# The first tap of each gate convolution: GpSimd replaced by VectorE as the planner's second choice

## The chip, the cores and the metric

One core of a Trainium2 chip runs the kernel. The metric is device time in microseconds for one execution. Engines: TensorE (PE; its weight loads are PEld), VectorE (DVE), ScalarE (ACT), GpSimd (POOL), and SyncE (SP), which issues the DMAs.

## What is computed

Attention with a local window of 96 positions and 8 global keys (2 batches, 8 heads, 768 positions, head size 64), and behind it two gated blocks with short convolutions along the sequence:

```python
x = attention(q, k, v)                        # [2, 768, 512]
# block 1: causal convolution of 5 taps over x
gate_pre = sum(conv_w[k] * x_padded[:, k:k + S, :] for k in range(5))
y = (sigmoid(gate_pre) * (x @ w_val)) @ w_out
# block 2: centred convolution of 3 taps over the hidden values
h = maximum(y @ w_in, 0.0)                    # d_ff = 1024
conv_out = sum(conv_w2[k] * h_padded[:, k:k + S, :] for k in range(3))
out = (h * sigmoid(conv_out)) @ w_out2
```

## The kernel before, in words

Channels lie on partitions, positions along the free dimension. The gated blocks are worked in four chunks, two for each batch (`PARTS`, lines 33 and following: 400 and 368 columns; 384 in the second block). For each chunk `hidden_inputs` splits x into a high and a low part (`gx`) and makes the four gates of block 1 (`z`), `values` multiplies by `w_val` and gates, `hidden` multiplies by the product of `w_out` and `w_in` (made on the chip in `weights`), and `gated` makes the eight gates of block 2 (`z2`) and the split operand `g2` of `project`. Every matmul of the blocks is three passes over split operands (`mm3`, lines 253 to 255); `split_ops` makes the high part on ScalarE (line 244) and the low part on VectorE (line 246).

`conv_gate` is called for both convolutions. Its first tap is a multiplication with one weight for each channel, `z = w0 * src`; each further tap adds `wk * src(k)` on VectorE (line 706), and a tanh on ScalarE (line 708) ends it. There are 4 x 4 first taps over x (tile names `z<-x,cw`) and 4 x 8 over h (`z<-h,cw`), 48 in all. Line 701 is the first tap on ScalarE, line 702 on GpSimd.

Nothing here is ordered by hand. Each step is put into a `Plan` with a cost for each engine that may do it. `lay` is a list scheduler: it goes forward in modelled time, and a step with several engines is taken by the one on which it would end first by the costs (`here`); a rank from a backward pass decides among ready steps. `issue` repeats backward and forward passes six times, keeps the pass with the earliest modelled end, and issues all steps in that order; each engine then runs its own steps strictly in that order and waits on semaphores. Costs and order are fixed when the kernel is built.

```python
def here(w, e):
    ends = {o: max(free[o], est[w]) + us for o, (us, _) in w.ways.items()}
    return back or min(ends, key=ends.get) == e
```

Other steps that the text names: scores (line 493), softmax on VectorE and ScalarE (504, 509), the probabilities' scaling on VectorE, GpSimd or ScalarE (530, 533, 536), their transposes on TensorE (563) and copies out of PSUM (567, 573), their product with v (588), the rounding of raw weights to f32 (272, 274 on GpSimd, 279, 282), the product of weights (337), the gate of block 1 (759), relu into h (800) with its edge columns from GpSimd (794 to 805), and the gate of block 2 (819).

Of the kernel before, what the change touches and what calls it, by code (L numbers as in the profile page):

```python
# [14 lines left out]
ALU = mybir.AluOpType  # L15
# [69 lines left out]
class Plan:  # L85

    LAG = {"PE": 0.2, "ACT": 0.15, "DVE": 0.15, "POOL": 0.15, "SP": 0.0, "AHEAD": 0.0}
    START = {"DVE": 0.4, "ACT": 1.2, "SP": 6.3}  # L90
# [130 lines left out]
def act_us(n, sbuf=True, scaled=False, sums=False):  # L221
    return 0.05 + 0.000834 * n + 0.042 * sbuf + 0.092 * scaled + 0.093 * sums


def dve_us(n, scaled=False):
    return 0.069 + 0.001042 * n + 0.061 * scaled
# [6 lines left out]
def pool_us(n):  # L233
    return 0.17 + 0.0013 * n
# [27 lines left out]
def to_f32(c, dst, raw, n, bufs, reads, token):  # L262
# [5 lines left out]
    def whole(): return high().bitcast(F32)  # L268
    def bits(): return dst().bitcast(I32)
# [3 lines left out]
    pl.add(  # L273
        "POOL", pool_us(n), lambda: nc.gpsimd.tensor_scalar(whole(), whole(), 0.0, 1.0, ALU.mult, ALU.mult),  # L274
        bufs, reads + [token], [tail],
# [120 lines left out]
def head_ways(c, n, out, d, h):  # L396

    nc, k = c.nc, -slope(h) / QKSCALE
    return {
        "POOL": (0.02 + pool_us(n), lambda: nc.gpsimd.tensor_scalar(out(), d, k, 1.0, ALU.mult, ALU.mult)),  # L400
        "ACT": (act_us(n), lambda: nc.scalar.activation(out(), d, AF.Copy, scale=k)),
# [35 lines left out]
def fast_attention(c, ap):  # L437
# [35 lines left out]
    def held(d, ts):  # L473
        return [d[t] for t in ts if t in d]

    for t in range(nt):
# [7 lines left out]
        for half in range(2):  # L484
# [40 lines left out]
            four = [("p", t, h) for h in range(4 * half, 4 * half + 4)]  # L525
            pl.add("POOL", 0.12, guard, [st], four, [("r", t, half)])
            pl.add("DVE", 0.2, invert, [st], [], [("r", t, half)])
            for h in range(4 * half, 4 * half + 4):
# [6 lines left out]
                def on_act(h=h, st=st, w=p[h], nk=nk):  # L535
# [3 lines left out]
                    "DVE", 0.22 + 0.00052 * nk, on_dve, [p[h], st], [("r", t, half)], [("p", t, h)],  # L539
                    POOL=(0.2 + pool_us(nk), on_pool), ACT=(act_us(nk, True, True), on_act),  # L540
                )
# [6 lines left out]
        if i == 0:  # L548
            pl.add("POOL", 0.4, first_keys, held(kq, [t]), [("kq", t)], ["gl"])
        elif i < NT - 1:  # L550
# [145 lines left out]
def conv_gate(c, z, width, src, n, w, taps, bufs, reads, token):  # L696


    nc, pl = c.nc, c.plan
    pl.add(  # L700
        "ACT", act_us(n, True, True), lambda: nc.scalar.activation(z(), src(0), AF.Copy, scale=w()[:, 0:1]), bufs, reads, [token],  # L701
        POOL=(pool_us(n), lambda: nc.gpsimd.tensor_scalar(z(), src(0), w()[:, 0:1], 1.0, ALU.mult, ALU.mult)),  # L702
    )
    for k in range(1, taps):
        def tap(k=k):
            nc.vector.scalar_tensor_tensor(z(), src(k), w()[:, k : k + 1], z(), ALU.mult, ALU.add)  # L706
        pl.add("DVE", dve_us(n, True), tap, bufs, reads, [token])
    pl.add("ACT", act_us(n), lambda: nc.scalar.activation(z(), z(), AF.Tanh, scale=0.5), bufs, [], [token])  # L708


def hidden_inputs(c, b, ch):


    nc, ring = c.nc, c.ring
    t0, n = PARTS[ch]
    xt = [("x", i) for i in range(max(0, t0 - K1 + 1) // P, (t0 + n - 1) // P + 1)]
    gx, z = [], []
    for d in range(NC1):
        g = ring["gx"].new()
        split_ops(  # L720
            c, lambda g=g: g.t[:, 0, :n], lambda g=g: g.t[:, 1, :n], lambda d=d: c.x[:, d, XP + t0 : XP + t0 + n],
            n, [g], xt, ("gx", b, ch, d),
        )
        gx.append(g)
    for d in range(NC1):
        zz = ring["z"].new()

        def src(k, d=d):
            return c.x[:, d, XP + t0 - K1 + 1 + k : XP + t0 - K1 + 1 + k + n]

        conv_gate(
            c, lambda zz=zz: zz.t[:, :n], CW, src, n, lambda d=d: c.c1w[:, :, d], K1, [zz], xt + ["cw"], ("z", b, ch, d)
        )
        z.append(zz)
    c.inputs[b, ch] = gx, z
# [73 lines left out]
def gated(c, b, ch, f, h):  # L809

    nc, pl = c.nc, c.plan
    z, g = c.ring["z2"].new(), c.ring["g2"].new()
    tk, zt = [("h", b, ch, f), ("h", b, ch, f, "edge")], ("z2", b, ch, f)
    conv_gate(
        c, lambda: z.t, CH, lambda k: h.t[:, k : k + CH], CH, lambda: c.c2w[:, :, f], K2, [z, h], tk + ["cw"], zt
    )

    def gate():
        nc.vector.scalar_tensor_tensor(z.t, z.t, 1.0, h.t[:, 1 : 1 + CH], ALU.add, ALU.mult)  # L819

    pl.add("DVE", dve_us(CH), gate, [z, h], tk, [zt])
    split_ops(c, lambda: g.t[:, 0], lambda: g.t[:, 1], lambda: z.t, CH, [g, z], [zt], ("g2", b, ch, f))
    c.g2.setdefault((b, ch), []).append(g)
# [223 lines left out]
```

## Time and profile before

| | |
|---|---|
| median of 3 runs | 284.13 us (283.84 to 284.21) |
| the profiled execution | 283.84 us, of which the span is 281.9 us |
| TensorE busy, share of the span | 269.6 us, 96% |
| VectorE | 232.2 us, 82% |
| ScalarE | 194.8 us, 69% |
| GpSimd | 90.0 us, 32% |
| mean granted clock of TensorE | 0.999 |

The span runs from the first instruction of the program to the last one's end. A share is an average over stages with different limits, so the stages are to be read one by one. Matmuls overlap and their ends are modelled, so a matmul's busy time is longer than its step from start to start.

### The profile page before, as it was taken

The numbers are of one execution on the slowest core, as the hardware profiler recorded it, in microseconds if no ns is written. First come the engines' busy times: TensorE is split into PE (matmuls) and PEld (weight loads), VectorE is DVE, ScalarE is ACT, GpSimd is POOL, SyncE is SP. The second block draws the span as 40 slices with busy tenths as digits, with TensorE's granted clock in tenths as the row PEclk, the third lists the DMA queues.
The fourth block names the chain that finished last, engine by engine and source line by source line (L and its number), as shares of the span: only waits on it lengthen the run. The fifth ranks groups of instructions, "written<-read, shape, count | busy, mean of one in ns | idle before, by whom it ended". The sixth has DMA issues, their size and how long they took to land.

```text
span 281.9 us, 5430 instructions
## 1 busy us (share of the span) xinstructions
PE 269.6 (96%) x1832; PEld 226.3 (80%) x1832; DVE 232.2 (82%) x587; ACT 194.8 (69%) x496; POOL 90.0 (32%) x199
## 2 busy tenths in 40 slices
PE   2889999999999999999999999999999999999993
PEld 2767675655458989999999999889999988899883
DVE  3989999999999999999999999999984654357600
ACT  2999989998678999886797456883473254544520
POOL 4635746346353336533256001140411000002000
PEclk9999999999999999999999999999999999999999
DMA  5983877446733431003300000100000020000121
GB/s 165 356 346 97 277 243 237 141 140 216 227 87 140 144 127 49 9 2 116 121 0 0 3 0 0 40 37 1 37 2 0 0 77 37 37 1 2 38 112 49
DMA packets 10420, 26.17 MB, mean 93 GB/s; under 512 B 1424, under 2 KB 2704, under 8 KB 10384
## 3 DMA queue, kind: packets, MB, share of 16 engines
q1 hardware_dynamic: 9968, 25.22, 26.4%
q10 hardware_dynamic: 416, 0.52, 0.5%
q8 instruction: 16, 0.26, 0.4%
q14 instruction: 20, 0.16, 0.2%
HBM read 22.59 MB, written 3.15 MB: 91 GB/s over the span
## 4 chain that ended last, share of the span: by engine, by line
PE 72%; DVE 21%; issue 3%; ACT 1%; DVEq 1%; POOL 0%
PE s L254 8%; PE s L255 8%; PE s L253 8%; PE f L253 7%; PE f L254 7%; PE f L255 7%; DVE p L504 5%; PE t L563 4%; PE x L588 4%; PE s L493 4%; DVE z L706 3%; DVE raw L279 3%; PE t L255 2%; PE x L255 2%; PE x L253 2%
## 5 line engine op out<-in xcount | busy, mean ns | idle before, releaser
L706 DVE SCALAR_TENSOR_TENSOR z<-h,cw,z 128x384 f32<-128x384 f32 x64 | 40.7, 642 | 12.8 <-ACT z L701 11.6
L509 ACT ACTIVATE p<-p,st 128x256 f32<-128x256 f32 (+1 forms) x96 | 46.0, 482 | 3.8 <-DVE st L504 2.9
L708 ACT ACTIVATE z<-z 128x384 f32<-128x384 f32 (+2 forms) x48 | 24.8, 523 | 26.3 <-DVE z L706 26.0
L706 DVE SCALAR_TENSOR_TENSOR z<-x,cw,z 128x400 f32<-128x400 f32 (+1 forms) x64 | 40.5, 666 | 0.1
L254 PE MATMUL s<-w,g 128*128 128x512 f32 (+1 forms) x104 | 39.2, 377 | 0.0
L255 PE MATMUL s<-w,g 128*128 128x512 f32 (+1 forms) x104 | 39.2, 377 | 0.0
L253 PE MATMUL s<-w,g 128*128 128x512 f32 (+1 forms) x104 | 39.1, 376 | 0.0
L337 PE MATMUL f<-w,w 128*128 128x512 f32 x64 | 31.9, 607 | 0.1
L563 PEld LDWEIGHTS t<-ident,p 128*128 128x128 f32 x176 | 20.0, 141 | 14.0 <-issue 4.3
L504 DVE CUSTOM_DVE_ANT_0 p<-s,B 128x256 f32<-128x256 f32 x80 | 30.9, 412 | 0.3 <-PE s L493 0.3
L563 PE MATMUL t<-ident,p 128*128 128x128 f32 x176 | 28.6, 281 | 2.1 <-ACT pts L567 1.0
L533 POOL TENSOR_SCALAR p<-p,st 128x256 f32<-128x256 f32 (+1 forms) x38 | 24.8, 658 | 12.4 <-DVE st L523 11.4
L253 PE MATMUL f<-gg,Wh 128*128 128x400 f32 (+1 forms) x80 | 27.7, 347 | 0.0
L255 PE MATMUL f<-gg,Wl 128*128 128x400 f32 (+1 forms) x80 | 27.0, 338 | 0.0
L254 PE MATMUL f<-gg,Wh 128*128 128x400 f32 (+1 forms) x80 | 27.0, 338 | 0.0
L702 POOL TENSOR_SCALAR z<-h,cw 128x384 f32<-128x384 f32 x11 | 9.7, 883 | 51.6 <-DVE z L706 31.0
L274 POOL TENSOR_SCALAR raw<-raw 128x512 f32<-128x512 f32 x24 | 19.4, 810 | 16.8 <-ACT m L272 8.6
L255 PEld LDWEIGHTS s<-w,g 128*128 128x128 f32 x104 | 19.5, 188 | 3.9
L246 DVE TENSOR_TENSOR g<-z,g 128x384 fp32r<-128x384 f32 x32 | 17.7, 564 | 5.9 <-ACT g L244 5.9
L253 PEld LDWEIGHTS s<-w,g 128*128 128x128 f32 x104 | 19.5, 188 | 2.8
L254 PEld LDWEIGHTS s<-w,g 128*128 128x128 f32 x104 | 19.5, 188 | 2.8
L244 ACT ACTIVATE g<-z 128x384 fp32r<-128x384 f32 x32 | 16.3, 518 | 7.8 <-DVE z L819 4.7
(126 smaller groups left out, 662.2 us busy)
## 6 DMA issues: line engine op xcount, KB each, us to landing
raw<-in_moe_w_out_dram SPq DMA_DIRECT2D x12, 512.0 KB, 3.4
raw<-in_moe_w_in_dram SPq DMA_DIRECT2D x8, 512.0 KB, 4.9
k<-in_kq_dram SPq DMA_DIRECT2D x7, 512.0 KB, 4.5
v<-in_v_dram SPq DMA_DIRECT2D x11, 256.0 KB, 4.2
out_dram<-o SPq DMA_DIRECT2D x11, 256.0 KB, 2.0
raw<-in_moe_w_val_dram SPq DMA_DIRECT2D x4, 512.0 KB, 3.4
kq<-in_kq_dram SPq DMA_DIRECT2D x3, 512.0 KB, 4.6
v<-in_v_dram SPq DMA_DIRECT2D x8, 64.0 KB, 3.0
```

What stands on the lines that cost most here:

```text
L246: "DVE", dve_us(n), lambda: nc.vector.tensor_tensor(lo(), src(), hi().bitcast(F32), ALU.subtract),
L253: nc.tensor.matmul(out, lh, rh, start=first, stop=False)
L254: nc.tensor.matmul(out, lh, rl, start=False, stop=False)
L255: nc.tensor.matmul(out, ll, rh, start=False, stop=last)
L274: "POOL", pool_us(n), lambda: nc.gpsimd.tensor_scalar(whole(), whole(), 0.0, 1.0, ALU.mult, ALU.mult),
L337: nc.tensor.matmul(ps.t, big["wot"].t.bitcast(F32)[:, e, cs], big[wi].t.bitcast(F32)[:, e, :], start=e == 0, stop=e == 3)
L504: nc.vector.tensor_tensor_reduce(w.t[:, :nk], sc, bias, -QKSCALE, 3.0e38, ALU.add, ALU.min, st.t[:, 0, h : h + 1])
L509: nc.scalar.activation(w.t[:, :nk], w.t[:, :nk], AF.Exp, bias=st.t[:, 0, h : h + 1], scale=-1.0, accum_out=st.t[:, 1, h : h + 1],)
L533: nc.gpsimd.tensor_scalar(w.t[:, :nk], w.t[:, :nk], st.t[:, 2, h : h + 1], 1.0, ALU.mult, ALU.mult)
L563: nc.tensor.transpose(o[:, z, n, :], p[2 * pr + z].t[:, n * P : (n + 1) * P], ident)
L706: nc.vector.scalar_tensor_tensor(z(), src(k), w()[:, k : k + 1], z(), ALU.mult, ALU.add)
L708: pl.add("ACT", act_us(n), lambda: nc.scalar.activation(z(), z(), AF.Tanh, scale=0.5), bufs, [], [token])
```

## The change

The second engine that may do a first tap is VectorE instead of GpSimd, with a cost of 0.15 us and 0.00052 us for each column; ScalarE stays the first choice in the text, with its cost of 0.184 us and 0.000834 us for each column. The costs are the planner's figures. The whole order is laid anew with them.

```diff
@@ def conv_gate(c, z, width, src, n, w, taps, bufs, reads, token):
     pl.add(
         "ACT", act_us(n, True, True), lambda: nc.scalar.activation(z(), src(0), AF.Copy, scale=w()[:, 0:1]), bufs, reads, [token],
-        POOL=(pool_us(n), lambda: nc.gpsimd.tensor_scalar(z(), src(0), w()[:, 0:1], 1.0, ALU.mult, ALU.mult)),
+        DVE=(0.15 + 0.00052 * n, lambda: nc.vector.tensor_scalar(z(), src(0), w()[:, 0:1], None, ALU.mult)),
     )
```

## Rows read from the trace of the kernel before

**Rows 1.** Stages: stretch, length, busy PE, PEld, DVE, ACT, POOL; clock, DMA, GB/s.
```profile
0.00:20.00 20.00, 13.23 (x134) 10.54 (x136) 14.48 (x74) 14.98 (x54) 9.73 (x33) 1.00 0.83 299
20.00:45.00 25.00, 25.00 (x238) 17.53 (x240) 23.80 (x80) 23.45 (x73) 14.86 (x28) 1.00 0.65 213
45.00:97.00 52.00, 51.10 (x355) 33.03 (x356) 51.42 (x142) 45.22 (x125) 24.54 (x39) 1.00 0.50 161
97.00:205.00 108.00, 108.00 (x728) 100.18 (x728) 106.25 (x229) 77.97 (x182) 36.00 (x73) 1.00 0.11 37
205.00:277.00 72.00, 72.00 (x384) 64.99 (x382) 35.77 (x65) 33.15 (x65) 4.88 (x28) 1.00 0.09 32
```

**Rows 2.** TensorE's waits: waiter, waited for, us in total, times, longest.
```profile
PE s L493 <- DMA x<-in_kq_dram: 4.8, 1, 4.8
PE t L563 <- ACT pts L567: 1.0, 2, 0.6
...
PE f L253 <- DVE z L759: 0.2, 1, 0.2
```

**Rows 3.** The last matmul in the timeline: start, us, engine, line, operation, tiles, shapes.
```profile
276.96 0.28 PE L255 MATMUL s<-w,g 128*128 128x256 f32 x1
```

**Rows 4.** TensorE's timeline around 93 and 96 us (in brackets: idle before, releaser).
```profile
92.90 0.60 PE L563 MATMUL t<-ident,p 128*128 128x128 f32 x4
93.25 0.43 PE L253 MATMUL f<-gx,wvh 128*128 128x400 f32 x1
...
95.52 0.60 PE L563 MATMUL t<-ident,p 128*128 128x128 f32 x4
96.35 0.45 PE L253 MATMUL f<-gx,wvh 128*128 128x400 f32 x1 [0.23 <-DVE z L759]
```

**Rows 5.** The first taps: count, shortest, median and longest in ns, first and last start.
```profile
L702 POOL TENSOR_SCALAR z<-h,cw x11: 585/787/1369, 110.7 to 260.0; 128x384 f32<-128x384 f32 x11
L702 POOL TENSOR_SCALAR z<-x,cw x9: 595/850/2651, 43.6 to 184.8; 128x400 f32<-128x400 f32 x7, 128x368 f32<-128x368 f32 x2
L701 ACT ACTIVATE z<-h,cw x21: 605/617/622, 142.0 to 263.4; 128x384 f32<-128x384 f32 x21
L701 ACT ACTIVATE z<-x,cw x7: 586/603/634, 96.0 to 181.5; 128x368 f32<-128x368 f32 x6, 128x400 f32<-128x400 f32 x1
```

**Rows 6.** First taps by stage: three of GpSimd (line 702), then one of ScalarE (701).
```profile
40.00:60.00 20.00, 2.92 (x4) 1.00 0.60 195
...
97.00:205.00 108.00, 14.70 (x13) 1.00 0.11 37
205.00:282.00 77.00, 1.76 (x3) 1.00 0.09 33
...
205.00:282.00 77.00, 6.05 (x10) 1.00 0.09 33
```

**Rows 7.** VectorE: one-tensor scaling (530) as in rows 5 and 4, later taps (706).
```profile
L530 DVE TENSOR_SCALAR p<-p,st x29: 274/347/716, 9.3 to 123.8; 128x256 f32<-128x256 f32 x23, 128x128 f32<-128x128 f32 x6
...
47.00 0.34 DVE L530 TENSOR_SCALAR p<-p,st 128x256 f32<-128x256 f32 x1
47.26 0.62 DVE L706 SCALAR_TENSOR_TENSOR z<-x,cw,z 128x400 f32<-128x400 f32 x1
...
L706 DVE SCALAR_TENSOR_TENSOR z<-h,cw,z x64: 603/618/990, 120.3 to 264.8; 128x384 f32<-128x384 f32 x64
...
L706 DVE SCALAR_TENSOR_TENSOR z<-h,cw,z 128x384 f32<-128x384 f32 x64 | 40.7, 642 | 12.8 <-ACT z L701 11.6
```

**Rows 8.** GpSimd's timeline at 185 us, its longest first tap.
```profile
184.82 2.65 POOL L702 TENSOR_SCALAR z<-x,cw 128x368 f32<-128x368 f32 x1 [2.46 <-DVE gg L246]
```

**Rows 9.** Timeline: the first operands of a projection written, and its first matmul.
```profile
141.42 1.81 DVE L246 TENSOR_TENSOR g<-z,g 128x384 fp32r<-128x384 f32 x3
...
143.96 0.39 PE L253 MATMUL s<-w,g 128*128 128x512 f32 x1
```

**Rows 10.** Groups from 97 to 205 us: busy us, mean ns, idle before.
```profile
L706 DVE SCALAR_TENSOR_TENSOR z<-h,cw,z 128x384 f32<-128x384 f32 x38 | 24.8, 658 | 0.4
```

## The prediction

> **What bounds the kernel now.** I read the busy time of each engine by stage first, then what TensorE waited for, then the starts of its matmuls. The stages [rows 1] show TensorE idle in three places only: 6.8 us of the first 20, of which 4.8 wait for the first keys [rows 2]; 0.90 us between 45 and 97 (52.00 less 51.10); and the last 5, after its last matmul starts at 276.96 [rows 3]. From 97 to 277 it is busy for 180.00 of 180 us, at a granted clock of 1.00. A busy matmul row can hide a wait, since ends are modelled, so I compared starts: four transposes at 92.90 are followed by the next matmul after 0.35 us, four at 95.52 only after 0.83, though the row shows 0.23 us of idle time there [rows 4]. A wait of 0.48 us shows as 0.23, so the 0.90 us between 45 and 97 stands for some 0.9 to 1.9 us of lost matmul time. After 97 no such hole is left.
>
> VectorE comes second: 51.42 of 52 us in the stage from 45 to 97 and 106.25 of 108 in the next, and then half idle (35.77 of 72) [rows 1]. ScalarE has 6.8 us free in the one and 30 in the other. GpSimd is used for a third to a half. So what the change can win on the path is the 0.9 to 1.9 us of waits between 45 and 97; what lies before 43 us runs ahead of the first convolution, and the tail is a copy and a store.
>
> **What the change removes.** Of the 48 first taps 28 run on ScalarE and 20 on GpSimd (11 over h, 9 over x) [rows 5]. The 20 take about 19.4 us of GpSimd: 2.92 for four between 40 and 60, none between 60 and 97, 14.70 for 13 between 97 and 205 [rows 6], and 1.76 for the last three. None of it is on TensorE's path: among TensorE's waits there is none for a tap; beside that for the keys they are for copies of transposed probabilities and for one gate [rows 2]. Removed time on the path: nothing. It takes GpSimd's in-order queue past up to 20 waits, and edge copies of h, raw rounding and probability scaling no longer queue behind a tap; GpSimd has room for them already, so I put this at 0, with 0 to 0.3 us of gain (one of TensorE's short waits).
>
> **What it adds.** The planner gives each tap to the engine on which it would end first, by 0.35 us for VectorE and about 0.50 for ScalarE at n = 384, and lays the lists anew. A tap on ScalarE is known: 0.60 to 0.62 us [rows 5]. On VectorE this form is not in the trace with 384 columns. From below: the same instruction over 256 columns takes 0.34 us and over 128 at least 0.27 [rows 7], so 384 columns would take 0.34 + 0.07 = 0.41 us (an estimate), and since the next instruction starts 0.26 us after the 0.34 us one [rows 7], it would hold the queue for about 0.33. From above: a later tap with two tensors takes 0.62 [rows 7]. I take 0.33, for the row it comes from is the same operation.
>
> How many go there? Where VectorE is full its list always holds something, and ScalarE, free for 6.8 and 30 us, often ends first; after 205 us VectorE is half idle and would take nearly all. Of the 48 taps 3 on GpSimd and 10 on ScalarE lie after 205 [rows 6], so 35 before. I take a third of them, 12 taps: 12 x 0.33 = 4.0 us onto an engine with 0.58 + 1.75 us idle in those stages. Bounds: none, and all 35, 11.6 us. Against it stands what contention gives back: the 64 later taps over h have a median of 618 ns and a mean of 642 [rows 7], so (642 - 618) x 64 = 1.5 us were lost, part of it to GpSimd.
>
> In one place GpSimd paid instead: the tap at 184.82 took 2.65 us against 0.59 for the shortest [rows 5, 8] and was held up by more than four times its own length. The Trainium skill ("SBUF — State Buffer", SBUF: two separate sides) says that VectorE and GpSimd take one port pair as a lock held for a whole instruction, and the other side blocks fully. By it 20 taps of 0.59 us would return up to 11.7 us of VectorE time, more than 12 taps cost; the rows of this trace bear out a small part of that, and TensorE's sum is the same by either.
>
> What covers the added VectorE time? Operands lie ready ahead of TensorE: the first projection group starts at 143.96 with operands that began to be written at 141.42 and took 0.60 each, so about 1.9 us ahead [rows 9]; after 205 VectorE has 36 us idle [rows 1]. A net 2.5 us (4.0 less 1.5), collected over 160 us and met by a list laid with it, mostly stays under that. If the cover goes, TensorE waits for the excess. On ScalarE the 13 + 4 moved taps cost at most 17 x 0.6 = 10.2 us in stages with 37 us free.
>
> The waits move too. A tap on VectorE waits for relu's h from ScalarE and for the edge that GpSimd writes, and everything later in VectorE's queue (splits, gates, weights' bits) waits with it. In return VectorE needs fewer first taps from ScalarE: its later taps over h now wait 12.8 us, 11.6 of them for that [rows 7], but only 0.4 us of it between 97 and 205 [rows 10]; the rest lies later, where VectorE is half idle and TensorE full. Worth nothing in the sum.
>
> **The sum.** Profiled execution 283.84 us = span 281.9 + 1.9 around it; that is the lowest of the three runs, and the median is 284.13. Removed from the path 0, added 0, waits between 45 and 97 as they are, with a new list moving them by about one tap (0.4 us) either way: 283.8 from the profiled execution, 284.1 from the median. I say 284.0.
>
> **The rivals.** Faster: the new list closes the waits between 45 and 97. For it: they are for ScalarE's and VectorE's copies and one gate, and fewer tied-up taps leave the lists freer. Against: only four of the 20 taps lie before 97, and in 40 to 60 [rows 6], well ahead of the wait at 96 [rows 4]. It gives 283.84 - 0.9 to - 1.9, so 282.0 to 282.9.
>
> Slower: VectorE becomes the bound between 45 and 97. The four taps over x that GpSimd now does between 40 and 60 go to VectorE, which has 0.58 us idle until 97. It decides from the second of them on (2 x 0.33 = 0.66). Gates and transposed copies then come later and TensorE, already waiting for them, waits longer: four taps cost 4 x 0.33 = 1.3 us, at most 4 x 0.62 = 2.5. That is 285.1, to 286.3. For it: VectorE is the fullest engine beside TensorE and the wait at 96 us is for its gate. Against: ScalarE has 6.8 us free there, and the taps are not urgent: they are done some 40 us before that gate.
>
> It doesn't do what it says: with VectorE always taken before 205, the taps go to ScalarE, which is hardly a change there: 17 x 0.6 us beside 37 us free. It gives 284.0 as well.
>
> By the skill's lock rule, VectorE would be the lighter for the change; with TensorE full from 97 on, that is again within the first rival's times, and I give it no chance of its own beyond it.
>
> **How the numbers follow.** About 0.2%, 0.57 us, is what a measurement can tell from no change here. Forecast 0.34 and its twin with the taps on ScalarE 0.08: within 0.2%, 0.42 together. Closed waits 0.30: faster. VectorE as the bound 0.28: slower. The range reaches from the middle of the faster rival, 282.5, to the middle of the slower one's, 285.6; some 2 in 10 lie outside.
>
> **What would show it.** TensorE's idle time between 45 and 97 near 0.9 us, and none from 97 to 277, with the last matmul starting at 276.4 to 277.4: forecast. No GpSimd instruction at the tap's line, and some taps of about 0.41 us on VectorE, most of them after 205. Wrong if TensorE shows a wait after 97, or if its first 45 us change: the whole list is laid anew, ranks included, and an early reordering is the part that I can't price from these rows.

## The result and the profile after

The changed kernel takes 286.24 us (median of 11 executions, 284.97 to 287.79), the kernel before beside it 284.17 us; the ratio is 1.0065, 95% interval 1.0045 to 1.0085. It is slower, clear of the 0.2% that can be told from no change, and outside the predicted range. The execution profiled below took 286.95 us, its span 285.1 us.

| | before | after |
|---|---|---|
| profiled execution, span | 283.84, 281.9 us | 286.95, 285.1 us |
| mean granted clock of TensorE | 0.999 | 0.993 |
| VectorE, ScalarE, GpSimd busy | 232.2, 194.8, 90.0 us | 235.8, 194.5, 78.9 us |
| the planner's own end of its list | 265.05 us | 264.78 us |

The last line is the planner's figure, no time of the chip: by its costs the new list is 0.27 us better.

The stages of after, to be laid beside [rows 1] (stretch, length, busy PE, PEld, DVE, ACT, POOL; clock, DMA, GB/s):

```profile
0.00:20.00 20.00, 13.86 (x112) 11.64 (x112) 13.28 (x69) 12.85 (x46) 9.31 (x32) 0.91 0.78 268
20.00:45.00 25.00, 23.74 (x259) 17.94 (x258) 22.80 (x85) 24.03 (x77) 11.66 (x25) 1.00 0.49 155
45.00:97.00 52.00, 49.79 (x349) 31.66 (x348) 49.92 (x140) 44.29 (x123) 20.76 (x35) 1.00 0.59 200
97.00:205.00 108.00, 108.00 (x720) 100.33 (x719) 106.41 (x232) 83.85 (x197) 33.74 (x63) 1.00 0.12 37
205.00:277.00 72.00, 72.00 (x372) 64.86 (x371) 42.99 (x81) 29.14 (x58) 3.47 (x25) 1.00 0.07 27
```

From 97 to 277 TensorE is as full as before, though VectorE carries 7.2 us more behind 205. What is lost lies ahead of 97: 1.26 us more idle time between 20 and 45, 1.31 more between 45 and 97, and, in the first 20 us, a granted clock of 0.91 and a late start, both told below. TensorE's waits (waiter, waited for, us in total, times, longest), beside [rows 2]:

```profile
PE s L493 <- DMA x<-in_kq_dram: 4.8, 1, 4.8
PE x L588 <- DMA v<-in_v_dram: 2.7, 2, 1.7
```

The second is new: twice the products with v wait for a load of v. In TensorE's timeline:

```profile
27.96 0.63 PE L563 MATMUL t<-ident,p 128*128 128x128 f32 x4
29.59 1.09 PE L588 MATMUL x<-pts,v 128*64 128x128 f32 x16 [1.00 <-DMA v<-in_v_dram]
...
54.19 0.60 PE L563 MATMUL t<-ident,p 128*128 128x128 f32 x4
56.53 1.09 PE L588 MATMUL x<-pts,v 128*64 128x128 f32 x16 [1.75 <-DMA v<-in_v_dram]
```

And the queue that issues the loads, ahead of the first of these waits:

```profile
17.82 6.92 SPq L468 DMA_DIRECT2D k<-in_kq_dram  x2
25.03 0.33 SPq L309 DMA_DIRECT2D raw<-in_moe_w_in_dram  x1
26.20 0.34 SPq L600 DMA_DIRECT2D v<-in_v_dram  x1
```

The first 32 rows of v are issued at 26.20, behind a key tile (the second of the pair, at about 24.4) and a weight row of 512 KB each. They overwrite rows that the product before still reads, so they can't go before it ends, at 26.16. TensorE wants them at 28.6 (29.59 less 1.00). The planner's cost for this small load is 0.4 us and 2.4 for landing, 2.8 in all; here it lands 3.3 us after its issue. The second one, issued at 51.34, lands after 5.1. In the kernel before the load for the same product was issued at 24.35, landed after 2.1 us and was wanted only at 27.77, since weight products stood between.

The clock, in single microseconds of after (columns as above):

```profile
11.00:12.00 1.00, 0.58 (x3) 0.29 (x2) 0.38 (x3) 0.38 (x2) 0.67 (x2) 1.00 1.12 391
12.00:13.00 1.00, 0.41 (x2) 0.21 (x2) 1.00 (x8) 1.00 (x6) 0.70 (x3) 1.00 1.02 415
...
14.00:15.00 1.00, 0.92 (x10) 0.67 (x10) 1.00 (x6) 1.00 (x6) 0.48 (x1) 0.87 1.03 415
15.00:16.00 1.00, 1.00 (x12) 1.00 (x12) 0.37 (x2) 1.00 (x5) 0.00 (x0) 0.50 1.01 389
16.00:17.00 1.00, 1.00 (x14) 1.00 (x12) 0.52 (x3) 0.85 (x3) 0.19 (x1) 0.50 1.05 393
17.00:18.00 1.00, 1.00 (x12) 0.87 (x10) 0.96 (x7) 0.60 (x2) 0.00 (x0) 0.50 0.91 348
18.00:19.00 1.00, 1.00 (x12) 0.74 (x12) 0.77 (x5) 0.15 (x1) 0.74 (x2) 0.93 0.57 115
```

For 3 us TensorE runs at the lower of its two levels, 1.2 in place of 2.4 GHz; shortly before, between 11 and 13, it had idled half of 2 us. In seven of the eleven executions the mean granted clock was 0.993 or 0.994 (286.06 to 287.79 us, median 286.88), in four 0.997 to 0.999 (284.97 to 286.17 us, median 285.01): the medians are 1.9 us apart. The drop isn't the whole spread, for the kernel before ranges from 283.74 to 285.86 us as well.

One microsecond of the profiled difference is lost before TensorE's order differs: its first six steps are the same in both kernels. The first matmuls run at the pace of the lower level, though the clock row shows 1.00 there: groups of four start 0.43 us apart, as they do at 15.39 with 0.50 granted, and the first transposes start at 11.03:

```profile
7.90 0.84 PE L493 MATMUL s<-x,k 64*128 64x128 f32 x4
8.33 0.84 PE L493 MATMUL s<-k 64*128 64x128 f32 x4
...
11.03 0.56 PE L563 MATMUL t<-ident,p 128*128 128x128 f32 x2
...
15.39 0.65 PE L493 MATMUL s<-k,k 64*128 64x128 f32 x4
15.81 0.64 PE L493 MATMUL s<-k 64*128 64x128 f32 x4
```

In the profile of the kernel before the pace rises earlier (the groups at 8.46 and 8.74 are 0.28 apart), and the same transposes start at 10.05:

```profile
10.05 0.44 PE L563 MATMUL t<-ident,p 128*128 128x128 f32 x2
```

The first run of the next section has the list of the kernel before, and starts them at 10.84. So executions of one list differ by 0.8 us here, and none of the microsecond is shown to come from the new list.

The taps themselves did what the change says. Twenty went to VectorE, 28 ran on ScalarE, none on GpSimd. Count with shortest, median and longest in ns, as in [rows 5], and then VectorE's by stage, as in [rows 6]:

```profile
L702 DVE TENSOR_SCALAR z<-h,cw x15: 408/421/427, 123.1 to 266.5; 128x384 f32<-128x384 f32 x15
L702 DVE TENSOR_SCALAR z<-x,cw x5: 396/416/528, 52.3 to 142.0; 128x400 f32<-128x400 f32 x3, 128x368 f32<-128x368 f32 x2
...
45.00:97.00 52.00, 0.96 (x2) 1.00 0.59 200
97.00:205.00 108.00, 2.47 (x6) 1.00 0.12 37
205.00:277.00 72.00, 5.05 (x12) 1.00 0.07 27
```

### The profile page after: what moved, and what is told of

Same layout as the page of the kernel before. It is cut to its first block, busy times and chain, and to the rows that moved or that the text cites. A ratio compares the mean times of both kernels' runs of the same rounds, so it can differ in the third digit from the quotient of the medians.

```text
span 285.1 us, 5462 instructions
## 1 busy us (share of the span) xinstructions
PE 270.8 (95%) x1832; PEld 229.6 (81%) x1832; DVE 235.8 (83%) x604; ACT 194.5 (68%) x499; POOL 78.9 (28%) x179
## 4 chain that ended last, share of the span: by engine, by line
PE 80%; DVE 9%; DMA 3%; ACT 3%; issue 2%; POOLq 1%; POOL 0%; SPq 0%; DVEq 0%; ACTq 0%
PE s L254 8%; PE s L255 8%; PE s L253 8%; PE f L253 8%; PE f L255 7%; PE f L254 7%; PE s L493 7%; PE x L588 7%; PE t L563 6%; DMA v<-in_v_dram 3%; PE t L253 2%; PE x L255 2%; PE t L255 2%; PE t L254 2%; PE x L253 2%; PE x L254 2%
## 5 line engine op out<-in xcount | busy, mean ns | idle before, releaser
L706 DVE SCALAR_TENSOR_TENSOR z<-h,cw,z 128x384 f32<-128x384 f32 x64 | 39.4, 623 | 1.6
L706 DVE SCALAR_TENSOR_TENSOR z<-x,cw,z 128x400 f32<-128x400 f32 (+1 forms) x64 | 39.4, 653 | 0.1
L337 PE MATMUL f<-w,w 128*128 128x512 f32 x64 | 31.1, 602 | 0.1
L274 POOL TENSOR_SCALAR raw<-raw 128x512 f32<-128x512 f32 x24 | 21.6, 903 | 23.3 <-ACT m L272 16.4
L588 PE MATMUL x<-pts,v 128*64 128x128 f32 x320 | 21.5, 277 | 3.1 <-DMA v<-in_v_dram 2.7
L588 PEld LDWEIGHTS x<-pts,v 128*64 128x64 f32 x320 | 17.4, 137 | 7.0 <-ACT p L509 3.2
L567 ACT ACTIVATE pts<-t 128x512 f32<-128x512 f32 (+1 forms) x35 | 19.5, 557 | 4.8 <-PE t L563 4.8
L255 PEld LDWEIGHTS s<-w,g 128*128 128x128 f32 x104 | 19.5, 188 | 3.9
```

Source lines behind the costliest of these rows:

```text
L255: nc.tensor.matmul(out, ll, rh, start=False, stop=last)
L337: nc.tensor.matmul(ps.t, big["wot"].t.bitcast(F32)[:, e, cs], big[wi].t.bitcast(F32)[:, e, :], start=e == 0, stop=e == 3)
L588: nc.tensor.matmul(o[z * D : (z + 1) * D, pr, :], vals(j, 2 * pr + z), pts[pr].t[:, z, n, :], start=n == 0, stop=n == len(js) - 1,)
```

## The experiments

Two theories went in. A: the loss is in the order that was laid anew for all engines, in the first 60 us. B: VectorE is too full for the taps it was given. Ratios are to the kernel before on the same chip, with 95% intervals.

### The old list, taps on VectorE in GpSimd's places

```diff
-        POOL=(pool_us(n), lambda: nc.gpsimd.tensor_scalar(z(), src(0), w()[:, 0:1], 1.0, ALU.mult, ALU.mult)),
+        POOL=(pool_us(n), lambda: nc.vector.tensor_scalar(z(), src(0), w()[:, 0:1], None, ALU.mult)),
```

> The lists of the kernel before, with the planner's costs for GpSimd kept, but the 20 first taps that stand in GpSimd's places are issued to VectorE there. Theory A (the loss is in the order that was laid anew, in the first 60 us; the engine of the tap costs nothing): within 0.2% of the kernel before, 283.6 to 284.8 us, and TensorE without a wait after 97 us. Theory B (VectorE is too full for the added taps, 20 x 0.33 = 6.6 us of its time): TensorE waits after 45 us and the time is that of the changed kernel, 285.5 to 287.

285.5 us, ratio 1.0039 (1.0024 to 1.0053): at the lower edge of B's range, above A's and short of the changed kernel's time. Neither theory is whole. With the same list each matmul can be compared with itself. The late start costs 0.79 us at the first transposes, before any tap. From the first tap on, at 44.4, TensorE falls back a little at several waits for VectorE and for what stands behind it. The first transposes and two of the waits:

```profile
10.84 0.44 PE L563 MATMUL t<-ident,p 128*128 128x128 f32 x2
...
64.91 0.44 PE L563 MATMUL t<-ident,p 128*128 128x128 f32 x2 [0.35 <-DVE pts L573]
...
126.14 0.66 PE L563 MATMUL t<-ident,p 128*128 128x128 f32 x4 [0.37 <-ACT pts L567]
```

In the kernel before these transposes start at 10.05, 63.46 and 124.23, so the lag is 1.45 us at the first wait and 1.91 at the second, where nothing waits any more afterwards. Of that 0.61 is there already at a product with v that starts at 41.23 and at 40.62 before, ahead of the first tap. So taps on VectorE do cost time in a list that wasn't laid for them: 1.3 us in this trace, 1.2 by the medians.

### The new list, taps on GpSimd in VectorE's places

```diff
-        DVE=(0.15 + 0.00052 * n, lambda: nc.vector.tensor_scalar(z(), src(0), w()[:, 0:1], None, ALU.mult)),
+        DVE=(0.15 + 0.00052 * n, lambda: nc.gpsimd.tensor_scalar(z(), src(0), w()[:, 0:1], 1.0, ALU.mult, ALU.mult)),
```

> The lists of the changed kernel, but the 20 taps that it gives to VectorE are issued to GpSimd in the same places. Theory A: as slow as the changed kernel, 285.0 to 287.0 us, with the same waits for loads of v near 28 and 55 us. Theory B: back to the kernel before, 283.7 to 284.8 us, since VectorE is freed of the taps.

287.17 us, ratio 1.0102 (1.0071 to 1.0133), a little above A's range. B falls as the cause of this loss: without a single tap on VectorE it stays whole, and both waits for v stand in its trace (2.1 us), with the clock at 0.91 in the first 20 us. The clock drop and the first of these waits also lie ahead of the changed kernel's first tap, at 52.3 us. From the trace of this run:

```profile
PE x L588 <- DMA v<-in_v_dram: 2.1, 2, 1.1
...
0.00:20.00 20.00, 13.86 (x112) 11.67 (x112) 13.30 (x69) 12.83 (x46) 9.29 (x32) 0.91 0.76 272
```

### The new choice behind the old beginning, 36 us and 18 us of planned time

The work is laid first with ScalarE or GpSimd; what starts ahead of the edge keeps its engine and its place in the order, and the rest is laid with the new choice.

```diff
         if laid:
+            self.as_before(EDGE)
...
-                    w.rank = -back[w] - w.cost + w.bias
+                    w.rank = -back[w] - w.cost + w.bias if w not in self.pin else 1e3 * self.pin[w] - 1e9
```

> The choice is that of the changed kernel (ScalarE or VectorE), but every step that the kernel before starts in its first 36 us of planned time (about the first 43 us on the chip) keeps the engine and the place that it has there; only the rest is laid anew. Theory A, in the form that the early order does it: 283.6 to 284.8 us, no wait for v before 40 us, TensorE's clock up by 10 us. Theory B: 285.5 to 287 us, since VectorE takes the taps as before.

> As the one kept to 36 us, but kept only for the first 18 us of planned time (about 20 to 25 us on the chip). If the late rise of TensorE's clock is all of the loss: 283.6 to 284.8 us. If the late loads of v are the larger part and recur in the new rest: 284.8 to 286 us with the clock up by 10 us. Theory B: 285.5 to 287 us.

Kept to 36: 283.91 us, ratio 0.9986 (0.9974 to 0.9997). Kept to 18: 283.61 us, ratio 0.9966 (0.995 to 0.9982). The loss is gone with the early order kept, and the second is faster than both kernels, with 19 first taps on VectorE. What lies behind the edges is a new draw of the list as well, so the gain can't be put down to the early order or to VectorE alone. The second gained more than was expected of it: late loads of v hardly recur (0.2 us in its trace), and between 45 and 97 TensorE idles 0.25 us where it idled 0.90 before [rows 1]:

```profile
PE x L619 <- DMA v<-in_v_dram: 0.2, 1, 0.2
...
45.00:97.00 52.00, 51.75 (x365) 34.03 (x364) 49.75 (x136) 45.34 (x126) 23.49 (x38) 1.00 0.47 162
```

### Two small loads of v left out

```diff
+            def first_rows(b=b, t=t):
+                if t not in (1, 4):
+                    nc.sync.dma_start(vs[t].t[0:GW], c.v[b, 0:GW].rearrange("s (a h) d -> s a h d", a=2))
...
+                "SP", dma_us(64), first_rows,
```

> The changed kernel with its lists unchanged, leaving out two of the eight small loads of v's first 32 rows (for the second and the fifth tile of the first batch), so those rows of v are wrong there. TensorE's waits for v near 28 and 55 us, 2.7 us in the trace of the changed kernel, should go. If they are half of the loss: 284.0 to 285.2 us, with the clock still at half speed near 15 to 18 us in some executions. If they were hidden by the next wait anyway: 286 to 287. If the wait near 55 us is for a whole tile of v in place of the small load, only the first goes, and the time falls by some 1 us to 285.2.

282.47 us, ratio 0.9943 (0.9922 to 0.9963): below the expected range, and lower by 3.8 us than the changed kernel's median, more than the 2.7 us that the waits show. The waits for v are gone from its trace. The executions fall into two groups, eight from 282.02 to 282.60 us with mean granted clocks of 0.996 to 0.998, and three from 284.26 to 284.51 with 0.990 to 0.992. The profiled one is of the second, and its clock is at half again:

```profile
14.00:15.00 1.00, 1.00 (x8) 0.67 (x9) 1.00 (x5) 1.00 (x6) 0.36 (x1) 0.50 1.00 397
15.00:16.00 1.00, 1.00 (x12) 1.00 (x12) 0.03 (x1) 1.00 (x5) 0.00 (x0) 0.50 1.06 401
16.00:17.00 1.00, 1.00 (x14) 1.00 (x12) 0.49 (x3) 0.51 (x1) 0.19 (x1) 0.50 1.07 406
```

So the two prices come apart, by medians of the executions with either clock (their number in brackets):

| | clock dropped | clock kept | clock drop costs |
|---|---|---|---|
| changed kernel | 286.88 us (7) | 285.01 us (4) | 1.9 us |
| two loads left out | 284.31 us (3) | 282.44 us (8) | 1.9 us |
| the loads cost | 2.6 us | 2.6 us | |

Beside the first row the kernel before took 284.17 us, beside the second, on its chip, 284.37. The 2.6 us fit the waits of 2.7, and 3 to 3.5 us at half speed are 1.5 to 1.8 us. With its clock kept the changed kernel is 0.8 us behind the kernel before, though the loads cost it 2.6, so the new list is some 1.8 better elsewhere. That is a difference; rows show a part: TensorE's other idle time ahead of 97, without the waits for the first keys and for v, is 2.1 us in place of 2.9 [rows 1, 2].

### TensorE's idle time filled ahead of the clock drop

```diff
+            def turn(pr=pr, pt=pt, p=p, nw=len(js), t0=t):
...
+                if t0 == 0 and pr in (1, 2):
+                    fill = c.psum.tile([P, 512], F32, tag="f", name="f")
+                    for _ in range(5):
+                        nc.tensor.matmul(fill[:, 0:P], ident, ident, start=True, stop=True)
```

> The changed kernel with its lists unchanged and ten matmuls of 128 columns more (identity by identity, into a bank that nothing reads) put where TensorE idles between 11 and 13 us, five ahead of each of two groups of transposes. If that idling is what goes before the drop of the granted clock to 0.5 near 15 us: clock 1.00 up to 20 us, and 0.8 to 1.6 us less than the changed kernel, 284.6 to 285.5 us, though work was added. If the drop has another cause: 286 to 287.5 us with the clock at 0.5 again.

287.64 us, ratio 1.0116 (1.0092 to 1.014). In the profiled execution the granted clock stays at 1.00 up to 28 us, as the first half of the expectation had it; but four executions of the changed kernel keep it without the added matmuls, so one profile doesn't show that they did it. The time didn't fall. TensorE now comes earlier to the same load of v, waits longer for it, and the clock drops there:

```profile
26.56 0.63 PE L567 MATMUL t<-ident,p 128*128 128x128 f32 x4
29.35 1.98 PE L592 MATMUL x<-pts,v 128*64 128x128 f32 x16 [2.16 <-DMA v<-in_v_dram]
...
28.00:30.00 2.00, 0.65 (x6) 0.69 (x8) 2.00 (x7) 1.19 (x5) 0.48 (x1) 0.75 0.03 7
30.00:32.00 2.00, 2.00 (x18) 1.64 (x14) 0.17 (x3) 0.00 (x0) 0.00 (x0) 0.50 0.58 207
32.00:34.00 2.00, 2.00 (x22) 1.44 (x20) 0.84 (x4) 1.53 (x4) 0.32 (x2) 0.89 0.14 55
```

The product starts at 29.35 in place of 29.59: the load, which lands 4.4 us after its issue here, sets that point, and what is won ahead of it is lost at it.

### Other lists of the same planner

The planner keeps the best of six passes by its own end. Here another pass is kept (no operation differs from the kernel named, but engines do: 16 to 21 first taps go to the second engine), or the planner reckons with 3.4 us of landing for a load:

```diff
-                if best is None or end < best[0]:
+                if n == 3:
```
```diff
-LANDING = 2.4
+LANDING = 3.4
```

> The kernel before with GpSimd as the second engine, but issued by the list of the planner's fourth pass (its own end 265.65) instead of the third (265.05). No operation differs. If the drawing of a list alone moves the time by as much as the change did: over 0.4% from the kernel before, to either side, most likely 285 to 287 us with a part of the difference before 60 us. If only the engine of the taps counts: within 0.2%, 283.6 to 284.9.

> The changed kernel by the list of the planner's fourth pass (its own end 265.41) instead of the second (264.78). If the list is what counts, not the taps on VectorE: another time than 286.2 by over 0.4%, with no order between the planner's own ends and the times; most likely 283.5 to 285.5, since the second pass lost to both a clock drop and two late loads. If the taps on VectorE cost the 0.65%: 285.5 to 287 again.

> The kernel before by the list of the planner's second pass (its own end 265.68, that of the third is 265.05). A third list with GpSimd as second engine: if GpSimd or VectorE decides, it stays within 0.3% of 284.4 us; if the list decides, 283.2 to 287.

> The changed kernel by the list of the planner's fifth pass, which the planner puts 1.6 us behind its best (266.42 against 264.78). If the planner's own end tells the chip's time: 1.6 us over the changed kernel, 287 to 288.5. If only waits for loads and the clock decide: 283 to 286.

> The changed kernel, planned with 3.4 us instead of 2.4 for a load's landing behind its transfer (with that 512 KB come to 4.7 us and 256 KB to 4.1, near the medians of the traces, 4.5 and 4.1). If late loads of v and the clock drops behind them are the loss, the planner now leaves room for them: no wait for v over 0.5 us and 282.8 to 284.2 us. If a new list is only another draw: anywhere from 283 to 287.

> The kernel before, GpSimd as second engine, planned with the same 3.4 us. If VectorE as second engine is itself worth something once the list is sound, this is slower than the changed kernel with 3.4 us by 0.3 us or more; if the second engine is worth nothing, the two lie within 0.6 us of each other or in the other order. Expected 283.2 to 285.2 us.

| list | planner's end | time, us | ratio (95%) |
|---|---|---|---|
| GpSimd, pass 3 (the kernel before) | 265.05 | 284.2 | 1 |
| GpSimd, pass 4 | 265.65 | 284.74 | 1.0031 (1.0005 to 1.0057) |
| GpSimd, pass 2 | 265.68 | 286.31 | 1.0066 (1.0042 to 1.009) |
| GpSimd, landing 3.4 | 266.34 | 286.32 | 1.0075 (1.0045 to 1.0105) |
| VectorE, pass 2 (the changed kernel) | 264.78 | 286.24 | 1.0065 (1.0045 to 1.0085) |
| VectorE, pass 4 | 265.41 | 283.2 | 0.9972 (0.9949 to 0.9994) |
| VectorE, pass 5 | 266.42 | 286.25 | 1.0064 (1.0041 to 1.0086) |
| VectorE, landing 3.4 | 265.77 | 284.85 | 1.0029 (1.0011 to 1.0047) |

Beside these lists the kernel before took 284.17 to 284.37 us; the ratios are to that. The planner's ends and the chip's times don't go together: the list with the best end is among the slowest, one 0.63 us behind it is the fastest, and one 1.64 us behind is level with it. Four lists with either engine lie from 284.2 to 286.3 and from 283.2 to 286.3. My expectations missed on both sides: the fourth pass of the kernel before moved less than I had said (0.31%), its second as much as the change did; the fourth with VectorE came out just below its range, and the fifth between its two ranges. A longer landing time removed the long waits for v of the changed kernel but cost others (with GpSimd, four waits for copies of transposed probabilities, 2.6 us), so 284.85 and 286.32 us both missed their ranges; there VectorE is ahead by 1.5 us, but that is one list each.

## Why the prediction was wrong, point by point

- *What bounds the kernel.* Held: TensorE is full from 97 us on, before, after and, but for at most 1.6 us, in every list that was run, and the whole difference between the two kernels arises ahead of it.
- *What lies before 43 us runs ahead of the first convolution.* This is the step that failed. It is true of the operations, and I took the time there as fixed. But ranks come from a backward pass over all the work, so a new choice for a tap at 43 us reorders TensorE from its seventh step on. The prediction named this as the part it couldn't price, and gave it no chance.
- *Waits move by about one tap, 0.4 us, either way.* The mis-sized term. Lists of one and the same set of operations differ by up to 2.1 us with GpSimd and 3.1 us with VectorE. The range should have been as wide as such draws, whose medians reach from 283.2 to 286.3 us.
- *The price of a tap on VectorE.* Held: 0.41 us estimated, 0.42 measured. The 0.33 that went into the sum, the time until the next instruction starts, was 0.32 to 0.34 at five of the eight taps before 205 us, and 0.43 to 0.46 behind it. The split came near: 12 before 205 us expected, 8 found, and 12 of the 13 behind it.
- *The contention given back.* Undercounted. The later taps over h went from a mean of 642 ns [rows 7] to 623 against a median of 618, 64 x 19 ns = 1.2 us of the 1.5. But the prediction looked at them alone: with the list kept (the first experiment), the durations of VectorE's other instructions fell by 3.9 us in all, by 1.3 over these taps. The lock rule of the Trainium skill ("SBUF — State Buffer", SBUF: two separate sides), by which up to 11.7 us were to come back, isn't borne out in this size for these taps.
- *What covers the added time.* Held where the list was laid for it; in the old list the same taps cost 1.2 us, all of it by 127 us.
- *The rival "slower".* The sign came, the mechanism didn't: VectorE is busy for 49.92 of 52 us between 45 and 97, less than before, and only two taps lie there.
- *The rival "faster"* was half at work: the new choice with a kept beginning closes the waits between 45 and 97, and is 0.34% faster.
- *Two slips in the working*, without weight in the sum: the tap at 184.82 was held up by 2.06 us (2.65 less 0.59), three and a half times its own length and not over four; and the middle of the slower rival is 285.7, not 285.6.

That late loads of v and the clock drop make up the loss is shown by the run without the loads, whose executions split by the clock as the changed kernel's do; the runs with the old beginning agree. Not settled is why the clock drops. In the traces with a drop it follows idle time of TensorE, but the list of pass 4 with VectorE idles as much at the same place and keeps 1.00 in its profiled execution (one of its twelve, of 286.44 us, had a mean clock of 0.984):

```profile
10.00:11.00 1.00, 0.48 (x3) 0.20 (x2) 1.00 (x7) 0.83 (x4) 0.86 (x3) 1.00 0.73 227
11.00:12.00 1.00, 0.41 (x2) 0.20 (x2) 1.00 (x7) 0.98 (x5) 0.57 (x3) 1.00 1.13 415
12.00:13.00 1.00, 0.45 (x4) 0.28 (x6) 1.00 (x5) 1.00 (x5) 0.37 (x1) 1.00 1.01 413
```

Nor is it settled what sets the moment at which the first matmuls come to full pace, or whether VectorE is the better second engine: the draws overlap.

## What to carry to other kernels

Where a planner lays the whole order, an edit to one step is a new draw of every list, and its price is first the spread between draws; measure that with other passes of the same planner before crediting or blaming the edit. To judge the edit itself, swap the engine within a fixed list and pin the rest, as here: in place it cost 0.4%, behind a pinned beginning it gained 0.3%, the latter in one list. Planner's ends that differed by up to 1.6 us said nothing here, where the model lacked the loads' measured landing and the clock. And before a lag between two traces is laid to an edit, look whether it is there already ahead of the first changed instruction.

## What the runs showed of the hardware

- TensorE idled for half of 2 us early in the run and shortly after ran 3 us at half the clock. By the mean granted clock this happened in seven of eleven executions of the changed kernel, and in three of eleven without the two loads. It cost 1.9 us in both, more than either wait for v (1.00 and 1.75).
- TensorE's first matmuls ran at half pace, and the moment of the rise differed between executions of one list: the same transposes started at 10.05 and at 10.84 us. The clock row showed 1.00 in that time.
- A first tap on VectorE took 0.42 us (19 of 20 from 0.40 to 0.43, one 0.53), while the same tap on GpSimd took from 0.59 to 2.65 us [rows 5].
- The same kind of 64 KB load landed after 2.1, 3.3, 4.4 and 5.1 us at the four places read here.
- Ten small matmuls put into TensorE's idle time ahead of a late load gained nothing: the median rose by 1.4 us. In the profile the wait for the load grew by 1.2 us and the clock fell at its end; how the 1.4 us come about isn't shown.
